# Reordering the opening of a one-core attention and feed-forward kernel: a weight load, two value chunks, two unread products and the banks of the first attention steps

## The chip, the cores and the metric

The kernel runs on one core of one Trainium2 chip. The metric is device time in microseconds from one launch; the time before is the median of three runs. All times inside the kernel are counted from the start of the span of one profiled execution, in which the engines appear as PE (TensorE), DVE (VectorE), ACT (ScalarE), POOL (GpSimd) and SP (the queue that issues stores).

## What is computed

The inputs are q, k and v of 4 batches, 8 heads, 768 positions and 64 channels, an 8 x 8 matrix for each batch and head, and three weights of 512 x 1536, 512 x 1536 and 1536 x 512. Cut to what matters:

```python
for _ in range(5):                      # P: 8 x 8 for each batch and head
    P = exp(P - max); P /= P.sum(-1); P /= P.sum(-2)
k_sorted = einsum('bhij,bhjcd->bhicd', P, k_blocks)   # 8 blocks of 96 rows
v_sorted = einsum('bhij,bhjcd->bhicd', P, v_blocks)
attn = softmax(q_block @ k_sorted_block.T / 8)        # 96 x 96 in each block
x = (attn @ v_sorted_block) as 3072 rows of 512
g = x @ w_gate
out = (g * sigmoid(g)) * (x @ w_val) @ w_out          # 3072 x 512, float32
```

## The kernel before

**The work.** A batch's 768 positions are cut into two halves of 384 rows, so the feed-forward part has eight steps of 384 rows (`ffn(0)` to `ffn(7)`). Each needs an `xt` tile: the attention output of half a batch, transposed, in four slices of 128 (two heads each). The attention of half a batch is four units, numbered 0 to 3 for the first half of batch 0. Unit u consists of

- `qk(0, u)`: eight score products into PSUM (line 332), then the exponentials on ACT (line 345 where one instruction covers both heads, line 343 where there is one for each head);
- `av(0, u)`: eight products of the exponentials with the mixed values (line 359), then on DVE a reciprocal (line 363) and a scaling into the tile `st` (line 365);
- `x_first(u)`: four transposes of `st` on PE (line 376) and a copy into slice u of `xt` (ACT for the first three, DVE for the last).

**Ahead of the units.** The queries, keys and values of batch 0 are transposed and mixed on PE in chunks: `q0_chunk` (line 274), `k0_chunk` (line 284), `v_chunk` (line 300, eight channels at a time for the values). Each chunk's PSUM tile is drained by ACT ("s", line 244) or DVE ("v", line 242). The keys' last chunk (`k0_chunk(32, 16, ...)`) is drained in two parts, the first by ACT for units 0 and 1, the second (`drain_rest`) by DVE for units 2 and 3. The values are first rearranged in SBUF into `vch` by copies on POOL (line 150) and ACT (line 148); POOL's third copy, 64 x 624, fills the channels from 40 up of rows 46 to 71.

**After the units.** `early(n, kcs)` (line 557) computes the first four feed-forward products (two columns of gate, two of value) slice by slice as the slices of `xt` arrive; the rest of `ffn(0)` (lines 410 and 428), the second half of batch 0 and all later batches follow in lists ordered by written-out due times.

**What sets the order.** The order of PE, POOL, DVE and ACT is the order of the calls, written by hand (`manual_schedule`). PE, DVE, ACT and POOL each run their own list in order; semaphores make them wait for each other. POOL issues all loads of this stretch (the DMA queue is fed in the order of its list): values, queries, keys, then the weights (`load_w`, line 136), first 256 columns of `wg` and of `wv`, and so on. A load waits for the landing of the one eight places ahead of it.

**PSUM.** Tags name the places: "a" and "b" are one tile each of two banks, "x" is one bank, and "gen" is three banks in rotation. A new tile of a tag waits until the old one has been read. `qk` with tag "gen" takes two "gen" banks, with "mixed" one "gen" and "x", with "a" or "b" the two-bank tile.

**Unread products.** `fill` (line 477) multiplies 128 x 128 by 128 x 512 zeros into a bank that nobody reads, and `wide_fill` (line 481) does it in float32.

Of the kernel before, what the change touches and what calls it, by code (L numbers as in the profile page):

```python
# [17 lines left out]
def kernel(  # L18
# [24 lines left out]
    TW = 4 * C  # L43
# [6 lines left out]
    wg_dram = moe_w_gate.rearrange("(kc p) f -> p kc f", p=128)  # L50
    wv_dram = moe_w_val.rearrange("(kc p) f -> p kc f", p=128)
# [22 lines left out]
    wg_sb = wpool.tile([128, NKC, DF], BF16)  # L74
    wv_sb = wpool.tile([128, NKC, DF], BF16)
# [59 lines left out]
    def load_w(sb, dram, lo, hi):  # L135
        nc.gpsimd.dma_start(out=sb[:, :, lo:hi], in_=dram[:, :, lo:hi])

    def load_gv(lo, hi):
        load_w(wg_sb, wg_dram, lo, hi)
        load_w(wv_sb, wv_dram, lo, hi)  # L140

    def copy_v(eng, pair, rows, s, n=4, d0=0, d1=D, cs=None):
        cs = cs or slice(s * (C // n), (s + 1) * (C // n))
        dst = vch3[rows, d0:d1, cs]
        src = (dense(v_tiles[0])[rows, cs, d0:d1] if rows == lowr else
               grouped(v_tiles[pair])[rows, s, :, d0:d1])
        if eng is nc.scalar:
            eng.copy(dst, src.transpose([0, 2, 1]))
        else:
            eng.tensor_copy(dst, src.transpose([0, 2, 1]))  # L150
# [16 lines left out]
    def load_q0(t):  # L167
        nc.gpsimd.dma_start(out=q0[t].rearrange("p c d -> p (c d)"), in_=q_runs[0, t])
# [6 lines left out]
        nc.gpsimd.dma_start(out=k0[rows], in_=k_nat[0, :, a * HC:(a + 1) * HC, :])  # L175
    copy_v(nc.gpsimd, 0, lowr, 0)
    copy_v(nc.gpsimd, 0, lowr, 3)
    load_w(wg_sb, wg_dram, 0, 256)
    copy_v(nc.gpsimd, 0, lowr, 0, d0=40, cs=slice(46, 72))
    load_w(wv_sb, wv_dram, 0, 256)  # L180
    load_q0(1)
    load_gv(256, 512)
    load_gv(512, 1024)
# [9 lines left out]
    def vt_tile(pair):  # L193
        if pair not in vts:
            t = vtp.tile([C, 2, H * NB, D + 8], BF16, name=f"vt{pair}", tag="vt")
            nc.vector.memset(t[:, :, :, D:D + 1].rearrange("p u n e -> p (u n) e"), 1.0)
            vts[pair] = t
        return vts[pair]
# [12 lines left out]
    def pair_tile(name, tag):  # L211
        return psum.tile([128, 1024], FP32, name=name, tag=tag)

    def bank_tile(name, tag="gen"):
        return psum.tile([128, 512], FP32, name=name, tag=tag, bufs=3 if tag == "gen" else 1)
# [24 lines left out]
    def drain(eng, dst, src):  # L240
        if eng == "v":
            nc.vector.tensor_copy(dst, src)  # L242
        else:
            nc.scalar.copy(dst, src)  # L244
# [3 lines left out]
    def kqt_tile(b):  # L248
        if b not in kqts:
            kqts[b] = kqp.tile([128, 2 * H2 * NB * C + 32], BF16, name=f"kqt{b}", tag="kqt")  # L250
        return kqts[b]
# [3 lines left out]
    def chunk_tile(name, n, tag):  # L255
        return pair_tile(name, tag) if n == 2 else bank_tile(name, tag)
# [12 lines left out]
    def q0_chunk(t, at, n, eng, tag):  # L269
        dst = kqt_tile(0)[:, GI * C:2 * GI * C].rearrange("p (g t r c) -> p t g r c", g=H2, t=2, c=QC)[:, t]  # L270
        tp = chunk_tile("tq0", n // 8, tag).rearrange("p (l g r) -> p l g r", l=n, g=H2)
        for lc in range(n):
            for two in range(2):
                nc.tensor.matmul(tp[two * D:(two + 1) * D, lc], lhsT=q0[t][:, at + lc, :],  # L274
                                 rhs=sel[:, two], start=True, stop=True)
        drain(eng, dst[:, :, :, at:at + n], tp.rearrange("p l g r -> p g r l"))

    def k0_chunk(at, n, eng, tag, parts=None):
        dst = kqt_tile(0)[:, 0:GI * C].rearrange("p (n a c) -> p a n c", a=2, c=HC)
        rm = rmix[0].rearrange("p a (g two) i -> p two a g i", two=2)  # L280
        tp = chunk_tile("tk0", n // 8, tag).rearrange("p (l a n) -> p l a n", l=n, a=2)
        for lc in range(n):
            for two in range(2):
                nc.tensor.matmul(tp[two * D:(two + 1) * D, lc].rearrange("p a (g i) -> p a g i", g=H2),  # L284
                                 lhsT=k0[:, at + lc, :], rhs=rm[:, two], start=True, stop=True)
        src = tp.rearrange("p l a n -> p a n l")
        if parts is None:
            drain(eng, dst[:, :, :, at:at + n], src)
            return
        drain(eng, dst[:, :, 0:parts, at:at + n], src[:, :, 0:parts])  # L290
        return lambda e: drain(e, dst[:, :, parts:, at:at + n], src[:, :, parts:])

    def v_chunk(b, at, n, eng, tag):
        rows = slice(0, 128) if b % 2 else lowr
        dst = vt_tile(b // 2)[:, b % 2]
        mix = rmix[b][rows, 0].rearrange("p a b -> p (a b)")
        tp = chunk_tile("tv", n // 8, tag).rearrange("p (l n) -> p l n", n=H * NB)
        for ld in range(n):
            col = (at + ld) * C
            nc.tensor.matmul(tp[:, ld, :], lhsT=vch[rows, col:col + 128], rhs=mix,  # L300
                             start=True, stop=True)
        drain(eng, dst[:, :, at:at + n], tp[0:C].transpose([0, 2, 1]))
# [35 lines left out]
    def exps(b, u, wide, pss):  # L338
        n = ecount[0] % 8
        ecount[0] += 2  # L340
        if wide is None:
            for two in range(2):
                nc.scalar.activation(e_all[:, n + two, 0:4 * C], pss[two][0:C, 0:4 * C], AF.Exp, scale=scale)
        else:
            nc.scalar.activation(e_all[:, n:n + 2, 0:4 * C], wide[0:C, :, 0:4 * C], AF.Exp, scale=scale)  # L345
        es[(b, u)] = [e_all[:, n, :], e_all[:, n + 1, :]]

    def qk(b, u, tag="b"):
        exps(b, u, *scores(b, u, tag))

    def av(b, u, tag="a"):
        half, g = divmod(u, H2)
        vt = vts[b // 2][:, b % 2].rearrange("p (h i) e -> p h i e", h=H)
        av_ps = pair_tile("av_ps", tag).rearrange("p (two n) -> p two n", two=2)
        o = av_ps.rearrange("p two (i e) -> p two i e", i=4)
        for two in range(2):
            e = es[(b, u)][two]
            for i4 in range(4):
                nc.tensor.matmul(o[:, two, i4, 0:D + 1], lhsT=e[:, i4 * C:i4 * C + 128],  # L359
                                 rhs=vt[:, 2 * g + two, half * 4 + i4, 0:D + 1],  # L360
                                 start=True, stop=True)
        r_sb = ssp.tile([C, 2, 4, 1], FP32, name="r_sb", tag="r")
        nc.vector.reciprocal(r_sb, o[0:C, :, :, D:D + 1])  # L363
        st = ssp.tile([C, 4, 2, D], BF16, name="st", tag="st")
        nc.vector.tensor_tensor(st.rearrange("p i two d -> p two i d"), o[0:C, :, :, 0:D],  # L365
                                r_sb.to_broadcast([C, 2, 4, D]), op=ALU.mult)
        sts[(b, u)] = st
# [105 lines left out]
    idle_ps = bank_tile("idle_ps", "x")  # L473

    def fill(tile, n):
        for _ in range(n):
            nc.tensor.matmul(tile, lhsT=warm_sb[:, 0:128], rhs=warm_sb, start=True, stop=True)
# [46 lines left out]
    k0_chunk(16, 8, "s", "gen")  # L524
    k0_chunk(24, 8, "v", "gen")
    drain_rest = k0_chunk(32, 16, "s", "a", 2 * NB)
    v_chunk(0, 56, 8, "s", "gen")
    v_chunk(0, 40, 8, "v", "gen")
    qk(0, 0, "b")
    v_chunk(0, 48, 8, "v", "x")  # L530
    drain_rest("v")
    qk(0, 1, "gen")
    av(0, 0, "b")
    qk(0, 2, "a")
    idle_ps = bank_tile("idle_ps", "x")
    fill(idle_ps, 1)
    av(0, 1, "b")
    xts[(0, 0)] = xtp.tile([128, H2, TW], BF16, name="xt0_0", tag="xt")
    qk(0, 3, "gen")

    def x_first(u, eng, tag):
        x_ps = xt_tile(tag, 1)[:, 0]
        x_to(x_ps, 0, u)
        drain(eng, xts[(0, 0)][:, u, :], x_ps.rearrange("p a b -> p (a b)"))

    x_first(0, "s", "gen")
    av(0, 2, "a")
    x_first(1, "s", "gen")
    av(0, 3, "b")
    first = {}  # L550

    def early(n, kcs):
        sb, m, name = ((wg_sb, 0, "g_ps"), (wv_sb, 0, "v_ps"), (wg_sb, 1, "g_ps"), (wv_sb, 1, "v_ps"))[n]
        if n not in first:
            first[n] = (bank_tile(name) if n < 3 else pair_tile(name, "a"))[:, 0:TW]
        for kc in kcs:
            nc.tensor.matmul(first[n], lhsT=sb[:, kc, ts(m, 128)], rhs=xts[(0, 0)][:, kc, :],  # L557
                             start=(kc == 0), stop=(kc == NKC - 1))

    early(0, (0,))  # L560
    early(1, (0,))
    x_first(2, "s", "x")
    early(3, (0,))
    early(2, (0,))
    early(0, (1,))
# [9 lines left out]
    value_out(0, 0, first[1])  # L575
    gate_out(0, 1, first[2])
    value_out(0, 1, first[3])
    q0_chunk(1, 0, 16, "s", "b")
    q0_chunk(1, 16, 8, "v", "x")
    vt_tile(1)  # L580
    nc.vector.tensor_copy(rmix[1][lowr, 1].rearrange("p h i -> p (h i)"), ident[lowr, lowr])
# [114 lines left out]
```

## Time and profile before

| | |
|---|---|
| median of 3 runs | 246.2 us (246.07, 246.2, 247.7) |
| the profiled execution | 245.73 us, of it 244.0 us span |
| mean granted TensorE clock | 0.993 of full |
| PE busy | 233.9 us |
| DVE busy | 155.2 us |
| ACT busy | 112.4 us |
| POOL busy | 54.8 us |

The span runs from the first to the last instruction; 1.73 us of the profiled execution lie outside it. Busy PE time includes the pipeline's own latency and the unread products. In the list of the 40 slices every digit is a tenth, for PEclk a tenth of full clock. The chain is followed back from the last instruction, and the groups give how often an instruction ran, its mean in ns, and what ended the idle time ahead of it.

### The profile page before, as it was taken

To read this page: it belongs to the slowest core of one execution; us is meant where nothing else is said; L and a number is where in the kernel's file an instruction comes from. 1 tells how busy PE (TensorE), PEld (TensorE's weight loads), DVE (VectorE), ACT (ScalarE), POOL (GpSimd) and SP (SyncE) were. 2 spreads that over 40 slices of the span, in tenths; PEclk is the share of its full clock that TensorE was granted. 3 is DMA by queue.
4 is the path that set the end of the run, shared out by engine and by line. 5 is a ranking of instruction groups with operands and counts; after the bars stand their busy time and mean duration, and the time that the engine had idled before them with its cause. 6 is when DMAs were issued, how large, how long until landed. Compare 5 with 4: busy or idle time off the path is not lost.

```text
span 244.0 us, 5910 instructions
## 1 busy us (share of the span) xinstructions
PE 233.9 (96%) x2468; PEld 137.6 (56%) x2490; DVE 155.2 (64%) x326; ACT 112.4 (46%) x190; POOL 54.8 (22%) x66
## 2 busy tenths in 40 slices
PE   7779999999999999999999999999999999999994
PEld 3376566676555565555555565565556555555543
DVE  6786699876664585867755845574675576445700
ACT  3985654476635444455543452254325334332312
POOL 5998228970006089000000000000000000000000
PEclk9997999999999999999999999999999999999999
DMA  5999999999926998644121212012111211110122
GB/s 97 211 133 188 207 210 211 206 204 196 171 79 98 219 172 101 130 80 95 46 75 35 60 58 77 2 59 63 32 43 46 75 36 43 43 43 3 43 86 86
DMA packets 40698, 24.76 MB, mean 102 GB/s; under 512 B 29408, under 2 KB 35424, under 8 KB 40672
## 3 DMA queue, kind: packets, MB, share of 16 engines
q0 software_dynamic: 20688, 14.16, 40.3%
q1 hardware_dynamic: 19840, 10.17, 15.9%
q8 instruction: 19, 0.31, 0.5%
q10 hardware_dynamic: 144, 0.07, 0.1%
q14 instruction: 7, 0.06, 0.1%
HBM read 28.32 MB, written 7.86 MB: 148 GB/s over the span
## 4 chain that ended last, share of the span: by engine, by line
PE 89%; DMA 4%; DVE 3%; issue 1%; POOL 1%; ACT 0%; DVEq 0%; POOLq 0%
PE v_ps L428 25%; PE g_ps L410 25%; PE o_ps L445 24%; DMA qk<-in_k_dram 4%; PE av_ps L359 3%; PE tkq L264 3%; PE qk L332 3%; PE tv L310 1%; PE o_ps L461 1%; PE tv L300 1%; PE tk L284 1%; PE x_ps L376 1%; DVE h L433 1%; PE g_ps L557 1%; PE v_ps L557 1%
## 5 line engine op out<-in xcount | busy, mean ns | idle before, releaser
L420 DVE SCALAR_TENSOR_TENSOR gs_sb<-th_sb,g_ps 128x384 bf16<-128x384 bf16 x96 | 53.1, 553 | 50.4 <-ACT th_sb L418 47.3
L428 PE MATMUL v_ps<-xt,wv_sb 128*128 128x384 bf16 x376 | 76.5, 326 | 0.5 <-DVE gs_sb L420 0.5
L410 PE MATMUL g_ps<-xt,wg_sb 128*128 128x384 bf16 x376 | 76.6, 325 | 0.1
L418 ACT ACTIVATE th_sb<-g_ps 128x384 bf16<-128x384 f32 x96 | 47.1, 491 | 57.5 <-PE g_ps L410 54.7
L445 PE MATMUL o_ps<-wo,h 128*128 128x512 bf16 x254 | 61.4, 379 | 1.5 <-issue 0.5
L433 DVE SCALAR_TENSOR_TENSOR h<-v_ps,gs_sb 128x384 bf16<-128x384 f32 x96 | 53.4, 556 | 8.2 <-PE tq L274 0.5
L428 PEld LDWEIGHTS <-wv_sb 128*128 128x128 bf16 x376 | 35.1, 97 | 23.5 <-issue 0.7
L410 PEld LDWEIGHTS <-wg_sb 128*128 128x128 bf16 x376 | 34.8, 97 | 23.4
L445 PEld LDWEIGHTS <-h 128*128 128x128 bf16 x276 | 26.0, 98 | 28.5
L450 ACT COPY o_sb<-o_ps 128x512 f32<-128x512 f32 x23 | 13.5, 586 | 49.3 <-PE o_ps L445 49.3
L150 POOL COPY vch<-v 64x1536 bf16<-64x1536 bf16 (+2 forms) x11 | 29.5, 2720 | 9.9 <-PE g_ps L410 8.1
L345 ACT ACTIVATE e_all<-qk 96x768 bf16<-96x768 f32 x30 | 23.3, 801 | 4.1 <-PE qk L332 4.1
L365 DVE TENSOR_TENSOR st<-av_ps,r_sb 96x512 bf16<-96x512 f32 x32 | 21.8, 681 | 0.3
L359 PEld LDWEIGHTS <-e_all 96*128 96x128 bf16 x256 | 12.4, 100 | 5.3 <-ACT e_all L345 0.6
L359 PE MATMUL av_ps<-vt,e_all 96*128 96x65 bf16 x256 | 13.5, 196 | 0.8 <-DVE vt L242 0.5
L244 ACT CAST vt<-tv 96x1024 bf16<-96x1024 f32 (+1 forms) x10 | 9.7, 966 | 4.2 <-PE tv L310 3.5
L363 DVE RECIPROCAL r_sb<-av_ps 96x8 f32<-96x8 f32 x32 | 6.4, 199 | 8.2 <-PE av_ps L359 8.2
L242 DVE CAST vt<-tv 96x512 bf16<-96x512 f32 (+1 forms) x9 | 8.1, 920 | 2.6 <-PE tv L310 1.8
L481 PE MATMUL idle_ps<-wide_sb 128*128 128x512 f32 x10 | 7.2, 866 | 1.5 <-DVE wide_sb L70 1.5
L242 DVE COPY oq_v<-o_ps 128x128 f32<-128x128 f32 x1 | 0.3, 292 | 9.3 <-PE o_ps L461 9.3
L395 POOL DMA_DIRECT2D q_scr<-in_q_dram x2 | 5.6, 2810 | 0.3 <-issue 0.3
L332 PE MATMUL qk<-kqt 64*128 64x96 bf16 x128 | 4.7, 208 | 0.4 <-DVE kqt L242 0.2
(87 smaller groups left out, 131.7 us busy)
## 6 DMA issues: line engine op xcount, KB each, us to landing
out_dram<-o_sb SPq DMA_DIRECT2D x23, 256.0 KB, 2.0
v<-in_v_dram POOLq DMA_DIRECT2D x4, 384.0 KB, 11.9
wo<-in_moe_w_out_dram POOLq DMA_DIRECT2D x3, 512.0 KB, 16.0
kqp<-in_k_dram POOLq DMA_DIRECT2D x2, 768.0 KB, 9.6
q_scr<-in_q_dram POOLq DMA_DIRECT2D x2, 768.0 KB, 17.4
v<-in_v_dram POOLq DMA_DIRECT2D x2, 768.0 KB, 9.8
wg_sb<-in_moe_w_gate_dram POOLq DMA_DIRECT2D x2, 512.0 KB, 11.8
wv_sb<-in_moe_w_val_dram POOLq DMA_DIRECT2D x2, 512.0 KB, 14.5
```

Of the source, the lines that this page charges most:

```text
L150: eng.tensor_copy(dst, src.transpose([0, 2, 1]))
L332: nc.tensor.matmul(pss[two][:, i4 * C:(i4 + 1) * C], lhsT=k_sb[lo:lo + D, k_at + at:k_at + at + 128], rhs=q_sb[lo:lo + D, q_at + at:q_at + ...
L345: nc.scalar.activation(e_all[:, n:n + 2, 0:4 * C], wide[0:C, :, 0:4 * C], AF.Exp, scale=scale)
L359: nc.tensor.matmul(o[:, two, i4, 0:D + 1], lhsT=e[:, i4 * C:i4 * C + 128], rhs=vt[:, 2 * g + two, half * 4 + i4, 0:D + 1], start=True, sto ...
L365: nc.vector.tensor_tensor(st.rearrange("p i two d -> p two i d"), o[0:C, :, :, 0:D], r_sb.to_broadcast([C, 2, 4, D]), op=ALU.mult)
L410: nc.tensor.matmul(g_ps, lhsT=wg_sb[:, kc, ts(m, 128)], rhs=xt[:, kc, :], start=(kc == 0), stop=(kc == NKC - 1))
L418: nc.scalar.activation(th_sb, g_ps, AF.Tanh, scale=0.5)
L420: nc.vector.scalar_tensor_tensor(gs_sb, th_sb, 1.0, g_ps, op0=ALU.add, op1=ALU.mult)
L428: nc.tensor.matmul(v_ps, lhsT=wv_sb[:, kc, ts(m, 128)], rhs=xt[:, kc, :], start=(kc == 0), stop=(kc == NKC - 1))
L433: nc.vector.scalar_tensor_tensor(h_tiles[n][:, m, :], v_ps, 0.5, gs_tiles.pop(m), op0=ALU.mult, op1=ALU.mult)
L445: nc.tensor.matmul(o_ps, lhsT=h_w[:, m, ts(t3, 128)], rhs=wo_sb[part][:, m % 4, :], start=(m == 0), stop=(m == NFC - 1))
L450: nc.scalar.copy(o_sb, o_ps)
```

## The change

Five edits, all in the first 30 us of the program:

1. The load of the first 256 columns of `wv` is issued ahead of POOL's third value copy (it was issued behind it).
2. `v_chunk(0, 40, ...)`, drained by DVE, comes ahead of `v_chunk(0, 56, ...)`, drained by ACT.
3. Two more unread products, 128 x 512 bf16, stand between `qk(0, 1)` and `av(0, 0)`, in a "gen" bank.
4. `qk(0, 2)` goes from "a" to two "gen" banks, `qk(0, 3)` from "gen" to "mixed".
5. `av(0, 1)` goes from "b" to "a", `av(0, 2)` from "a" to "b", `av(0, 3)` from "b" to "a"; the fourth early product goes from "a" to "b", and the next query chunk from "b" to "a".

```diff
     copy_v(nc.gpsimd, 0, lowr, 0)
     copy_v(nc.gpsimd, 0, lowr, 3)
-    load_w(wg_sb, wg_dram, 0, 256)
+    load_gv(0, 256)
     copy_v(nc.gpsimd, 0, lowr, 0, d0=40, cs=slice(46, 72))
-    load_w(wv_sb, wv_dram, 0, 256)
     load_q0(1)
...
     drain_rest = k0_chunk(32, 16, "s", "a", 2 * NB)
+    v_chunk(0, 40, 8, "v", "gen")
     v_chunk(0, 56, 8, "s", "gen")
-    v_chunk(0, 40, 8, "v", "gen")
     qk(0, 0, "b")
     v_chunk(0, 48, 8, "v", "x")
     drain_rest("v")
     qk(0, 1, "gen")
+    fill(bank_tile("idle_ps"), 2)
     av(0, 0, "b")
-    qk(0, 2, "a")
+    qk(0, 2, "gen")
     idle_ps = bank_tile("idle_ps", "x")
     fill(idle_ps, 1)
-    av(0, 1, "b")
+    av(0, 1, "a")
     xts[(0, 0)] = xtp.tile([128, H2, TW], BF16, name="xt0_0", tag="xt")
-    qk(0, 3, "gen")
+    qk(0, 3, "mixed")
...
     x_first(0, "s", "gen")
-    av(0, 2, "a")
+    av(0, 2, "b")
     x_first(1, "s", "gen")
-    av(0, 3, "b")
+    av(0, 3, "a")
...
-            first[n] = (bank_tile(name) if n < 3 else pair_tile(name, "a"))[:, 0:TW]
+            first[n] = (bank_tile(name) if n < 3 else pair_tile(name, "b"))[:, 0:TW]
...
-    q0_chunk(1, 0, 16, "s", "b")
+    q0_chunk(1, 0, 16, "s", "a")
     q0_chunk(1, 16, 8, "v", "x")
```

`load_gv(lo, hi)` calls `load_w` for `wg` and then for `wv`.

## The prediction

> **What bounds the kernel now.** I read the page first: PE has hardly a gap, and the chain that ended last is PE almost throughout. The one flaw is in the fourth slice of the granted clock.
>
> ```profile
> PE 233.9 (96%) x2468; PEld 137.6 (56%) x2490; DVE 155.2 (64%) x326; ACT 112.4 (46%) x190; POOL 54.8 (22%) x66
> ...
> PEclk9997999999999999999999999999999999999999
> ...
> PE 89%; DMA 4%; DVE 3%; issue 1%; POOL 1%; ACT 0%; DVEq 0%; POOLq 0%
> ```
>
> So from some 24 us on PE sets the end, and a step that comes there earlier moves the whole rest earlier by as much, as long as loads and copies keep up. The change lies ahead of that. Second view, stretches of 3.41 us (columns: stretch, length, busy us and count of PE, PEld, DVE, ACT, POOL, then clock, DMA share, GB/s):
>
> ```profile
> 6.23:9.64 3.41, 2.43 (x6) 0.76 (x5) 2.56 (x13) 3.35 (x5) 3.33 (x2) 1.00 1.07 214
> 9.64:13.05 3.41, 3.01 (x117) 2.30 (x117) 2.58 (x9) 3.07 (x3) 3.41 (x3) 1.00 0.92 187
> 13.03:16.44 3.41, 2.75 (x125) 2.46 (x120) 2.63 (x5) 2.69 (x5) 3.41 (x5) 1.00 0.88 103
> 16.44:19.85 3.41, 2.29 (x53) 1.68 (x53) 2.77 (x5) 2.91 (x6) 3.41 (x6) 1.00 1.21 194
> 19.85:23.26 3.41, 3.41 (x41) 2.63 (x41) 2.58 (x6) 2.00 (x5) 3.01 (x22) 0.50 1.32 179
> ```
>
> The clock is halved for exactly one such stretch, right after the one in which PE was least busy (2.29 us; with 2.43 or more in a stretch the next one kept full clock). Third view, PE in order of time, which shows where those gaps are (start, duration, idle before and its releaser):
>
> ```profile
> 17.01 0.39 PE L332 MATMUL qk<-kqt 64*128 64x96 bf16 x8
> 17.95 0.40 PE L359 MATMUL av_ps<-vt,e_all 96*128 96x65 bf16 x8 [0.55 <-DVE vt L242]
> 18.55 0.34 PE L332 MATMUL qk<-kqt 64*128 64x96 bf16 x8 [0.20 <-DVE kqt L242]
> 18.83 0.39 PE L477 MATMUL idle_ps<-warm_sb 128*128 128x512 bf16 x1
> 19.48 0.40 PE L359 MATMUL av_ps<-vt,e_all 96*128 96x65 bf16 x8 [0.26 <-DVE st L365]
> ```
>
> The chain of waits says the same: ACT and DVE stand behind PE's gaps here, and from 19.48 to 25.71 the chain is PE without a break, most of it at half clock.
>
> ```profile
> 17.21 0.69 DVE vt L242
> 17.90 0.60 DVE kqt L242
> ...
> 18.64 0.70 DVE st L365
> ...
> 19.48 0.40 PE av_ps L359 x8
> ```
>
> **The change, part by part.**
>
> *Load of `wv` ahead of the third copy.* POOL's rows: issue of `wg` 11.87 to 12.65, copy 12.65 to 13.92, issue of `wv` 13.84 to 14.60. Now the issue comes at 12.65 and the copy at 13.42 to 14.69. The copy's first reader, the value chunk at 15.85, has 1.1 us to spare; `q0` and the later issues keep their times (the same two pieces of work stand ahead of them). Landing of `wv` (4.4 us after issue, at 18.2) moves to about 17.1; its reader stands at 22.06 before and, below, at 21.1, so it is hidden either way. The keys land at 13.7, and `wv`'s issue ends at 13.4; the `wg` load issued 0.8 us ahead of it already stood behind the keys without a visible cost. Worth 0.
>
> *Value chunk order.* DVE's two value drains start at 16.52 and 17.21. The first can now start at 16.29 (its products are done 0.24 earlier). The second needs the products of 16.78 to 17.17, which stand behind `qk(0, 0)` at 16.60, which waits for ACT's key drain (15.96 to 16.55). So it starts at 17.21 as before: 0. ACT's own value drain comes 0.08 later, the exponentials of unit 0 end at 17.88 instead of 17.80, still ahead of DVE's drain at 17.90.
>
> *Two products.* They start at 17.2 (their bank is free at 17.11) and take 0.60 (row L477 at 10.31: two in 0.60), to 17.8, inside the gap that ends at 17.95. Cover left: 0.1. At half clock two would take some 1.0 and push `av(0, 0)` by 0.3; the row at full clock is nearest, so 0. What they buy is the clock: below.
>
> *Banks.* `av(0, 1)` waited for the scaling of unit 0 (ends 19.34) because both used "b". In "a" it needs DVE's second key drain (18.50) and the exponentials of unit 1 (18.26 and 18.64), so it follows the unread product directly: 18.83 + 0.22 = 19.05, 0.43 earlier. `qk(0, 2)` waits for DVE's key drain (18.50) in any banks: 18.55 as before; its exponentials become two of 0.48 (0.86 for the pair, row L343) instead of one of 0.81: +0.04. `qk(0, 3)` finds "mixed" free and follows at 19.29 (19.81).
>
> *The steps after that, clock at full.* I carry the rows forward, with PE to ACT or DVE 0.04, back to PE 0.06 (0.1 where the scaling releases the transposes), and each engine in its order:
>
> | | before | after | what it then waits for |
> |---|---|---|---|
> | unit 1 scaled (DVE) | 20.85 | 20.42 | `av(0, 1)` |
> | unit 3 exponentials end | 21.21 | 20.53 | ACT in order |
> | first transposes | 20.24 | 19.47 | exponentials of unit 2, first half |
> | unit 2 scaled | 22.16 | 21.31 | DVE in order |
> | second `xt` copy ends | 22.03 | 21.35 | ACT in order |
> | unit 3 scaled | 22.99 | 22.19 | DVE in order |
> | third transposes | 22.38 | 21.41 | unit 2 scaled |
> | fourth transposes | 23.63 | 22.32 | unit 3 scaled, third copy |
> | fourth `xt` copy ends | 24.36 | 23.05 | DVE |
> | last early product starts | 25.39 | 24.08 | seven products at 0.16 |
>
> Sum: **-1.3 us**. Of it about 0.5 comes from the banks alone (`qk(0, 3)` 0.52 earlier, after which PE is the chain in both), 0.8 from the clock. The ends: -0.5 if the clock falls as before, and for the clock alone at most half of 3.41, 1.7, which DVE and ACT in the table cut to 0.8.
>
> *Does the clock stay?* In the stretch 16.44 to 19.85 the gaps close: 0.55 to 0.1 by the products, 0.26 to 0 by the bank. Busy goes from 2.29 to about 3.0, above the 2.43 and 2.75 that kept it. In the next stretch the table leaves PE one gap, 20.13 to 20.50, so 3.0 again. Shifted edges make it worse: 17.4 to 20.8 holds 0.1, 0.2 and 0.4 of gaps, 2.75, still a value that kept the clock. In another execution the edges can lie elsewhere, so this is likely, not sure.
>
> The Trainium skill, page "TensorE: Matmul & The Clock Gate", section "Why this matters for your kernels", says that only PE gaps over about 3 us bring the half clock back. By that, gaps of 0.55 us would not be the cause, the products would cure nothing, and the sum would be -0.5 (rival 1). The trace disagrees: the clock fell with no gap over 0.55 us ahead of it.
>
> *Does the gain arrive?* Weights: the second half-load of `wv` (columns 512 on) is issued at 17.34 and lands 12.2 later, 29.5; its reader moves from 31.27 to 30.0. The next pair lands at 35.7 for a reader at 37.9, then 36.6. The narrowest is POOL's rearrangement of batch 1's values:
>
> ```profile
> 38.33 11.29 POOL L150 COPY vch<-v 64x1536 bf16<-64x1536 bf16 x4
> ...
> 51.09 0.63 PE L300 MATMUL tv<-rmix,vch 128*128 128x64 bf16 x16
> ```
>
> It ends at 49.62 and starts after a load lands, not after PE; the reader moves from 51.09 to 49.8. The gain just passes, and about 1.4 us is the cap there (1.7 if the earlier `wv` brings the later loads forward by 0.3).
>
> **Rivals.**
>
> 1. *The clock falls in the same place.* For it: one execution shows one fall, and 2.43 against 2.29 is a narrow mark. Against: busy 3.0. Then only the banks count: -0.5, 245.7.
> 2. *The clock falls one stretch later* (slower). If the gap at 20.13 to 20.50 and the short transposes leave too little work, the half clock lies on 23.3 to 26.7, where PE is busy without a pause (3.41 of 3.41 in that stretch): +1.7 against -1.3, +0.4, 246.6. It decides when busy in 19.85 to 23.26 drops under 2.43; I have 3.0. The same page, section "Part 1: The HAM clock gate", says that the window runs free of the kernel's start; no single execution can show that.
> 3. *The moved steps find another wait*, and the change does not do what it says: ACT, in order, has 0.86 of exponentials for each of three units in a row, and DVE 0.9 for each `av`; if these are already the bound, nothing moves: 246.2. Against it: ACT idles 0.39, 0.60 and 0.92 between 18.5 and 23, and DVE 0.59 and 0.38.
>
> **How the numbers follow.** The profiled execution took 245.73 (244.0 of span), 0.5 under the median 246.2. The sum gives 244.4 on its own time and 244.9 on the median, and I give 244.9. Chances: forecast 0.66, rival 1 0.19, rival 2 0.10, rival 3 0.05. The forecast's own range is 244.1 (1.6 off the profiled time) to 245.4 (gain 0.8). The range to hold 8 in 10 takes in rivals 1 and 3: 244.1 to 246.3. All cases lie within 1% (243.7 to 248.7, about what a measurement of this kernel can tell from no change): 0.91. Faster needs 2.5 us, more than the cap of 1.7: 0.05. Slower by 2.5 us needs the clock to fall twice or a load to come late: 0.04.
>
> **What would show it.** Right: granted clock 1.00 from 6.2 us to the end; `av(0, 1)` at about 19.05, right behind the unread product; the fourth `xt` copy ending near 23.05; the query chunk (L273) near 24.3; PE's later order the same, 1.3 us earlier; span near 242.7. Wrong: a 0.50 stretch anywhere (rivals 1, 2); `av(0, 0)` later than 18.1 (products too long); PE idle ahead of batch 1's first value chunk, released by POOL; the first value chunk later than 15.9, released by POOL's third copy.

## The result, and the profile after

The changed kernel takes **245.47 us** in the median (22 runs, 244.16 to 249.71), the kernel before on the same chip 246.6 us (22 runs, 245.32 to 248.55). The ratio is 0.9945 [0.9919, 0.997]; it leaves out the changed kernel's three longest runs (248.45 us and more), which count as disturbed, and with them the two medians give 0.9954. The forecast was 244.9 us, 1.3 us under the kernel before; 1.1 us were measured. The profiled execution took 244.4 us with a span of 242.6 (the prediction had 244.4 on its own time and 242.7).

The page of the changed kernel, the granted clock in 40 slices:

```profile
PEclk9999999999999999999999999999999999999999
```

The 7 in the fourth slice is gone. The stretches of the changed kernel, first two counted from this execution's own rise to full clock (at 7.6 us; more on that rise below), then one with the edges of the weak stretch before (columns: stretch, length, busy us and count of PE, PEld, DVE, ACT, POOL, then clock, DMA share, GB/s):

```profile
14.42:17.84 3.42, 2.97 (x106) 2.22 (x99) 2.59 (x5) 2.74 (x6) 3.42 (x6) 1.00 1.32 188
17.84:21.25 3.41, 2.93 (x60) 2.22 (x59) 3.14 (x9) 3.05 (x8) 3.21 (x7) 1.00 1.28 182
...
16.44:19.85 3.41, 3.04 (x65) 2.05 (x64) 2.94 (x7) 3.05 (x8) 3.41 (x6) 1.00 1.19 189
```

PE is busy 2.9 to 3.0 us in each, where 3.0 was forecast, and the clock stays at 1.00. (Busy figures of PE can be a little low: in the other traces the pages count some 2470 products for some 2490 weight loads, so a few products have no record. In this trace both counts are 2492.) PE in order of time, changed kernel (line numbers are one lower than before):

```profile
17.30 0.61 PE L476 MATMUL idle_ps<-warm_sb 128*128 128x512 bf16 x2
17.96 0.40 PE L358 MATMUL av_ps<-vt,e_all 96*128 96x65 bf16 x8
18.57 0.34 PE L331 MATMUL qk<-kqt 64*128 64x96 bf16 x8 [0.20 <-DVE kqt L241]
18.84 0.39 PE L476 MATMUL idle_ps<-warm_sb 128*128 128x512 bf16 x1
19.07 0.41 PE L358 MATMUL av_ps<-vt,e_all 96*128 96x65 bf16 x8
...
24.30 0.95 PE L273 MATMUL tq<-sel,qk 128*64 128x64 bf16 x48
```

The two unread products fill 17.30 to 17.91, and `av(0, 0)` starts at 17.96 (17.95 before): hidden. `av(0, 1)` starts at 19.07 instead of 19.48, with no wait on `st`. The query chunk starts at 24.30; before, it was 25.64, so this execution is 1.34 us ahead there, and its span is 1.4 us shorter.

One trace is one execution. The mean granted clock of each run tells more: 1.00 means that the clock never fell ("held"), about 0.99 that it lay at half for some 3.4 us, 0.986 or less for longer. Runs in each class, with the median us (the chips are called A, B and C; that of the 22 runs is not on record):

| kernel | runs | held | one fall | more |
|---|---|---|---|---|
| before, chip A | 35 | 2 (245.53) | 14 (246.03) | 19 (247.37) |
| before, chip B | 31 | 3 (244.92) | 14 (245.93) | 14 (247.13) |
| before, chip C | 11 | 0 | 3 (246.42) | 8 (247.30) |
| changed | 22 | 12 (244.53) | 6 (246.61) | 4 (248.47) |
| changed, chip C | 6 | 4 (245.04) | 0 | 2 (247.5) |

So the change moves the share of runs that hold from 5 of 77 to 16 of 28. It doesn't make every run hold. Held times are compared on one chip only, since the same kernel can hold at 244.30 us on one and at 244.84 on another (the kernel with four wide products, below). The question for the experiments is which edit does which, and what the remaining falls are.

### The profile page after: what moved, and what is told of

It is laid out like the page before. It is cut to its first block, busy times and chain, and to the rows that moved or that the text cites. A ratio compares the mean times of both kernels' runs of the same rounds, so it can differ in the third digit from the quotient of the medians.

```text
span 242.6 us, 5936 instructions
## 1 busy us (share of the span) xinstructions
PE 234.8 (97%) x2492; PEld 136.7 (56%) x2492; DVE 155.1 (64%) x326; ACT 112.3 (46%) x191; POOL 54.8 (23%) x66
## 4 chain that ended last, share of the span: by engine, by line
PE 90%; DMA 4%; DVE 3%; POOL 1%; issue 1%; ACT 0%; DVEq 0%; POOLq 0%
PE v_ps L427 25%; PE o_ps L444 25%; PE g_ps L409 25%; DMA qk<-in_k_dram 4%; PE av_ps L358 3%; PE tkq L263 3%; PE qk L331 3%; PE tv L309 1%; PE o_ps L460 1%; PE tv L299 1%; PE tk L283 1%; DVE h L432 1%; PE g_ps L557 1%; DVE gs_sb L419 1%; PE x_ps L375 1%
## 5 line engine op out<-in xcount | busy, mean ns | idle before, releaser
L444 PE MATMUL o_ps<-wo,h 128*128 128x512 bf16 x276 | 64.4, 379 | 0.0
L344 ACT ACTIVATE e_all<-qk 96x768 bf16<-96x768 f32 x29 | 22.5, 801 | 3.7 <-PE qk L331 3.7
L358 PE MATMUL av_ps<-vt,e_all 96*128 96x65 bf16 x256 | 13.0, 193 | 0.1
L148 ACT COPY vch<-v 64x640 bf16<-64x640 bf16 (+2 forms) x3 | 4.8, 1602 | 0.2 <-DMA v<-in_v_dram 0.2
```

The lines of the kernel that those rows point to most:

```text
L444: nc.tensor.matmul(o_ps, lhsT=h_w[:, m, ts(t3, 128)], rhs=wo_sb[part][:, m % 4, :], start=(m == 0), stop=(m == NFC - 1))
```

## The experiments

**Theory.** The clock falls after a stretch with too little PE work; the two products put the work there, the new banks shorten the path by 0.5 us, and the other edits do nothing. **Rivals:** the banks close enough of the gap by themselves, and the products are idle work; or the earlier load of `wv` gives the gain; or the falls come from somewhere else altogether.

### One part taken away or done alone

Changed kernel without the two products:

```diff
-    fill(bank_tile("idle_ps"), 2)
     av(0, 0, "b")
```

> The changed kernel without the two unread products; the load order, the value chunk order and the new banks stay. Theory 1 (the clock falls after a stretch of 3.41 us in which PE had too little to do): the 0.5 us gap ahead of av(0, 0) is open again, busy time in the sparsest stretch drops back to about 2.6 us, the clock falls in nearly every run, and only the 0.5 us of the banks is left: 0.998 of the kernel before. Theory 2 (gaps this short do not touch the clock, the products are idle work): as fast as the changed kernel, 0.9945 of the kernel before, with the clock falling as often as there.

Measured: 244.77 us, ratio 0.995 [0.9918, 0.9983]; of 12 runs 7 held (244.51), 3 had one fall (246.6), 2 more. The theory, which had the clock fall in nearly every run, fails here: without the products the kernel holds about as often as with them (16 of 28, on other chips). A stretch of this trace:

```profile
15.85:19.26 3.41, 2.35 (x64) 1.99 (x64) 2.77 (x5) 3.04 (x7) 3.41 (x6) 1.00 1.19 190
```

PE busy is 2.35, hardly more than the 2.29 after which the clock fell before, and the clock held. On the same chip, A, 2 of 35 runs of the kernel before held, so the edits that are left (banks, load order, chunk order) do something for the clock.

Kernel before, with the two products alone:

```diff
+    fill(bank_tile("idle_ps"), 2)
     av(0, 0, "b")
```

> The kernel before with nothing but the two unread products ahead of av(0, 0). Theory 1: the 0.55 us gap closes, the 0.26 us gap ahead of av(0, 1) stays, busy in the sparsest stretch is about 2.7 us, and the clock holds in part of the runs; in those the span is about 0.8 us shorter than before (243.2), av(0, 1) still at 19.48. Mean about 0.998 of the kernel before. Theory 2: nothing moves, 1.000, clock 0.993 as before.

Measured: 245.25 us, ratio 0.9972 [0.9946, 0.9998]; 8 of 12 held (245.02), 4 had one fall (246.72). So the products alone raise the held share too, from 2 of 35. Held runs are 0.4 to 0.55 us longer than those of the three kernels with new banks on this chip (244.47 to 244.61): the banks' share of the sum.

Changed kernel with the load of `wv` back behind the third copy:

```diff
-    load_gv(0, 256)
+    load_w(wg_sb, wg_dram, 0, 256)
     copy_v(nc.gpsimd, 0, lowr, 0, d0=40, cs=slice(46, 72))
+    load_w(wv_sb, wv_dram, 0, 256)
```

> The changed kernel with the wv load issued behind the third value copy again. If the load order is worth nothing, as I costed it: as fast as the changed kernel (0.9945 of the kernel before); the first wv load lands at 18.2 instead of 18.1 and the later loads 0.5 to 1.9 us later (the changed kernel had them that much earlier than before), POOL's copies of batch 1 end near 49.6 instead of 48.0, and their reader at about 49.8 waits at most 0.1. If the earlier loads carry part of the gain: 0.2 to 0.5 us slower than the changed kernel, with PE idle ahead of batch 1's first value chunk or ahead of a weight.

Measured: 244.99 us, ratio 0.9948 [0.9916, 0.9981]; 7 of 12 held (244.47), 4 one fall (246.62), 1 more. The held time is that of the kernel without the products on the same chip (244.51, with the load moved), so the load order is worth nothing that these runs could show. This trace caught one of the falls. PE in order of time at its start, then its stretches:

```profile
1.47 4.45 PE L481 MATMUL idle_ps<-wide_sb 128*128 128x512 f32 x6 [1.47 <-DVE wide_sb L70]
7.79 0.17 PE L484 MATMUL idle_ps<-vch 64*8 64x8 bf16 x1 [1.87 <-ACT vch L148]
7.88 3.55 PE L481 MATMUL idle_ps<-wide_sb 128*128 128x512 f32 x4
```

```profile
4.75:8.16 3.41, 1.54 (x5) 0.55 (x4) 2.29 (x12) 1.90 (x4) 1.68 (x1) 1.00 1.01 199
8.16:11.57 3.41, 3.35 (x9) 0.90 (x10) 2.43 (x11) 3.23 (x3) 3.41 (x2) 0.50 1.06 214
...
14.98:18.39 3.41, 1.97 (x98) 1.75 (x91) 1.92 (x4) 1.72 (x4) 3.41 (x6) 1.00 1.18 146
```

The fall is not where the prediction looked. The chip starts the program at a low clock and rises at a time that varies. The clock column does not show this start (it reads 1.00 from 0 us); the products' durations do: in the trace of the changed kernel one float32 instruction takes 1.06 us ahead of the rise and 0.59 us behind it. The three wide products are six such instructions. Here they took 4.45 us, in the traces of before and after 5.17 and 5.49 (the earlier the rise, the shorter). After an early rise the three wide products end at 5.92, PE idles 1.87 us until the values' first copy, the stretch holds 1.54 us of work, and the next 3.41 us run at half clock (the four instructions at 7.88 take 3.55 us; 1.98 in the trace of before). The last row is a stretch with 1.97 us of work after which the clock stayed.

Changed kernel with four more unread products:

```diff
+    fill(bank_tile("idle_ps", "x"), 2)
     k0_chunk(0, 8, "s", "x")
...
-    fill(bank_tile("idle_ps"), 2)
+    idle_gen = bank_tile("idle_ps")
+    fill(idle_gen, 2)
     av(0, 0, "b")
+    fill(idle_gen, 1)
     qk(0, 2, "gen")
...
     av(0, 2, "b")
+    fill(bank_tile("idle_ps"), 1)
     x_first(1, "s", "gen")
```

> The changed kernel with four more unread products in gaps that its trace still shows: two ahead of the first key chunk (gap 0.44), one ahead of qk(0, 2) (0.20), one ahead of x_first(1) (0.22). Theory 1: the changed kernel's single runs show a mean clock of 1.00 in some and 0.99 in others, since the edges of the stretches differ; with the gaps closed nearly all runs have 1.00, the best times stay near 244.2, and the median falls by 0.5 to 1 us, to 0.991 of the kernel before. Theory 2: the share of runs with a fallen clock stays about a half, and the time is that of the changed kernel or up to 0.3 longer where a product delays what stands behind it.

Measured: 244.73 us, ratio 0.9945 [0.9918, 0.9972]; 10 of 12 held (244.61), 2 had one fall. More than 16 of 28, but a share of 12 runs can't be read closely, and two falls remain.

### The early gap made smaller too

One more wide product ahead of the values' copy (`wide_fill(3)` to `wide_fill(4)`) takes from the early gap. With it, the two products can be judged with fewer early falls. First the changed kernel with four:

```diff
-    wide_fill(3)
+    wide_fill(4)
```

> The changed kernel with four instead of three wide float32 products at the start. In the trace of e3 the clock rose at 4.8 us, the three products ended at 5.7, PE then had nothing until 7.6, and the clock fell from 8.2 to 11.6. Theory 1 (the falls that the changed kernel still has in 10 of 22 runs are of that kind: an early rise ends the wide products early): the fourth product fills that gap, at least 10 of 12 runs hold a mean clock of 0.997 or more, median 244.5, 0.991 of the kernel before. Rival (they come from the sparse stretch between 13 and 20 us): the share stays near one half, 0.994.

Measured: 244.29 us, ratio 0.9906 [0.9873, 0.9938]; **8 of 8 held**. Its PE at the start and two of its stretches:

```profile
1.47 5.97 PE L480 MATMUL idle_ps<-wide_sb 128*128 128x512 f32 x8 [1.47 <-DVE wide_sb L70]
7.58 0.17 PE L483 MATMUL idle_ps<-vch 64*8 64x8 bf16 x1
```

```profile
6.08:9.49 3.41, 3.27 (x9) 1.05 (x7) 2.53 (x13) 3.25 (x5) 3.24 (x2) 1.00 1.06 213
16.32:19.73 3.41, 2.94 (x70) 2.22 (x71) 2.94 (x7) 3.06 (x7) 3.41 (x6) 1.00 1.12 174
```

In this trace no wait stands ahead of the small product at 7.58 any more: the fourth wide product ends just there. That depends on the rise. In four of the seven traces with four wide products a wait of 0.36 to 1.06 us is left there, and in one with a late rise (at 7.65 us; the kernel with the old chunk order, below) the fourth product ends late and the small one starts at 8.15.

The same without the two products (the removal of the first experiment and this line together):

> As e5, without the two unread products of the change. With the early falls out of the way this tells what the two products do. If they hold the clock in the stretch from 16.4 us, as I forecast: clear falls near 19 us come back in a third of the runs or more, and the median is 0.5 to 1 us above that of e5. If the new banks alone close enough of the gaps: the same share and the same time as e5, within 0.2 us.

Measured: 245.3 us, ratio 0.9958 [0.9927, 0.999]; 4 of 12 held (244.62), 6 one fall (245.71), 2 more. With 8 of 8 against 4 of 12 on one chip, the products do hold the clock once the fourth wide product is there.

The kernel before with four wide products:

> The kernel before with four instead of three wide products. Its own runs have two falls of the clock (mean clock 0.985, 247.4 us) in about half the cases, one (0.993, 246.05) in 14 of 35. Theory 1: the early fall goes, the one at 19.9 us stays; nearly all runs have one fall, median 246.1, 0.997 of the kernel before. Rival: no effect, half of the runs with two falls.

Measured: 246.42 us, ratio 0.9986 [0.9953, 1.0018]; 3 of 12 held (244.78), 3 one fall (246.15), 6 more. I had put the longer falls of the kernel before down to the early gap beside the later one. That idea falls: they go on with the fourth wide product, and this trace, of 246.68 us, shows one:

```profile
15.61:19.02 3.41, 2.44 (x58) 1.78 (x57) 2.78 (x6) 2.98 (x6) 3.41 (x6) 1.00 1.14 172
19.02:22.43 3.41, 3.25 (x44) 2.66 (x45) 2.14 (x7) 2.10 (x5) 3.17 (x22) 0.50 1.33 185
22.43:25.84 3.41, 3.41 (x19) 1.85 (x17) 0.80 (x2) 0.60 (x2) 1.20 (x3) 0.50 1.25 207
```

One fall can last two stretches: after 3.25 us of work in a half-clock stretch the clock did not come back, after 3.41 it did.

All extra products and four wide:

> e4 (four more unread products in the gaps at 13.2, 18.4 and 20.3 us) with the fourth wide product as well. Theory 1: all runs hold the clock, median 244.6; the products of e4 cost 0.1 in runs that hold it, so it is level with e5 or 0.1 slower where e5 holds everywhere, and faster in the mean where e5 still has falls.

Measured: 244.97 us, ratio 0.9938 [0.9912, 0.9964]; 12 of 12 held, at 244.97, where the kernel with two products and four wide holds at 244.30 on the same chip. The four more products keep nothing that the two don't. The held run is 0.67 us longer, though 0.1 was expected; with three wide products, on chip A, the same four cost 0.1 (244.61 against 244.47 and 244.51).

### Repeats, and the last two edits

The changed kernel once more, on chip C:

> The changed kernel as it is, beside the three others on one chip. Expected as in its own 22 runs: about half of the runs with a mean clock of 0.997 or more near 244.5, the others 2 us longer or more; 0.9945 of the kernel before in the median.

Measured: 245.25 us, ratio 0.9947 [0.9901, 0.9993]; 4 of 6 held (245.04), 2 had more than one fall. Its trace caught one of these. PE at the key chunk, then the stretches:

```profile
13.66 1.59 PE L283 MATMUL tk<-rmix,qk 128*64 128x64 bf16 x89 [0.34 <-DMA qk<-in_k_dram]
16.63 0.29 PE L283 MATMUL tk<-rmix,qk 128*64 128x64 bf16 x7 [1.39 <-issue]
```

```profile
15.51:18.92 3.41, 1.94 (x48) 1.47 (x49) 1.56 (x4) 1.96 (x4) 3.41 (x6) 1.00 1.22 193
18.92:22.33 3.41, 3.38 (x48) 2.59 (x49) 2.35 (x5) 2.34 (x7) 3.17 (x22) 0.50 1.33 180
```

PE stalled 1.39 us after 89 of 96 key products, waiting for nothing that the profile shows. That left 1.94 us of work in the stretch, in spite of the two products, and half clock followed for two stretches (to 25.74). One of the two products has no record in this trace, so the true figure may be some 0.2 us higher.

The kernel with four wide products once more:

> The changed kernel with four wide products at the start, once more, beside the changed kernel itself. If the fourth product takes the early fall away: no run under 0.997, 0.991 of the kernel before, below the changed kernel by the share of its runs with a fall times 2 us, that is 0.8 to 1 us in the mean. If e5's 8 runs were chance: falls in some of the runs.

Measured: 244.84 us, ratio 0.9905 [0.9874, 0.9935]; 6 of 6 held. Its median is under that of the changed kernel on this chip (245.25), and all 14 of its runs on two chips held, so it is the version to keep; the intervals of the two ratios overlap.

The same with the value chunks in their old order:

```diff
+    v_chunk(0, 56, 8, "s", "gen")
     v_chunk(0, 40, 8, "v", "gen")
-    v_chunk(0, 56, 8, "s", "gen")
```

> e5 with the two value chunks in the old order. As I costed it the order is worth nothing, since DVE's second drain starts at 17.21 either way: level with e5 within 0.2 us, DVE's two drains back to back, av(0, 0) at the same distance from the first key chunk. If the earlier first drain counts: 0.2 to 0.7 us slower.

Measured: 244.87 us, ratio 0.9908 [0.9877, 0.9939]; 6 of 6 held. The held time is level with 244.84: the chunk order is worth nothing that these runs could show. DVE of this kernel, then of the changed kernel:

```profile
16.91 1.38 DVE L241 CAST vt<-tv 96x512 bf16<-96x512 f32 x2 [0.86 <-PE tv L299]
```

```profile
16.30 0.69 DVE L241 CAST vt<-tv 96x512 bf16<-96x512 f32 x1 [0.56 <-PE tv L299]
17.22 0.69 DVE L241 CAST vt<-tv 96x512 bf16<-96x512 f32 x1 [0.23 <-PE tv L299]
```

The trace of the old order runs some 0.4 us later from the key chunk on (14.02 instead of 13.72). In it the two drains stand back to back; in the new one the first is earlier and DVE idles 0.23 us before the second, which still starts at 17.22 (17.21 before).

Last, the kernel with four wide products and the old banks:

```diff
-    qk(0, 2, "gen")
+    qk(0, 2, "a")
...
-    av(0, 1, "a")
+    av(0, 1, "b")
...
-    qk(0, 3, "mixed")
+    qk(0, 3, "gen")
```

(and `av(0, 2)`, `av(0, 3)`, the fourth early product and the next query chunk back likewise).

> e5 with the old tags of qk(0, 2), qk(0, 3), av(0, 1) to av(0, 3), the fourth early product and the query chunk; load order, chunk order, two products and four wide products stay. With the clock held the banks are worth 0.5 us by my sum (av(0, 1) waits for the scaling of unit 0 again, 0.4 later): held runs 0.5 us above e5. By the stretch rule the 0.26 gap comes back and some runs may fall. If the banks' worth was only in the clock: held runs level with e5.

Measured: 245.41 us, ratio 0.9933 [0.9902, 0.9964]; 6 of 6 held. Against 244.84 on the same chip, in held runs alone, the banks are worth 0.57 us (the lowest of the six, 245.16, is above the highest of the other six, 245.02). PE in order of time, old banks first, then the new ones:

```profile
19.00 0.34 PE L331 MATMUL qk<-kqt 64*128 64x96 bf16 x8 [0.20 <-DVE kqt L241]
19.27 0.39 PE L476 MATMUL idle_ps<-warm_sb 128*128 128x512 bf16 x1
19.92 0.40 PE L358 MATMUL av_ps<-vt,e_all 96*128 96x65 bf16 x8 [0.26 <-DVE st L364]
```

```profile
18.40 0.34 PE L331 MATMUL qk<-kqt 64*128 64x96 bf16 x8 [0.20 <-DVE kqt L241]
18.68 0.39 PE L476 MATMUL idle_ps<-warm_sb 128*128 128x512 bf16 x1
18.90 0.41 PE L358 MATMUL av_ps<-vt,e_all 96*128 96x65 bf16 x8
```

From `qk(0, 2)` to `av(0, 1)` it is 0.92 us in the old banks and 0.50 in the new: with the wait on `st` gone, `av(0, 1)` comes 0.42 sooner, against the 0.43 of the prediction.

With four wide products, the two edits in question make a table of two by two (runs that held of all runs; the upper row is from chip B, the lower left from C, the lower right from both):

| | old banks | new banks |
|---|---|---|
| without the two products | 3 of 12 | 4 of 12 |
| with them | 6 of 6 | 14 of 14 |

Here the products hold the clock and the banks don't. With three wide products the picture is another one: products alone 8 of 12, banks with the load and chunk order 7 of 12, all of them 16 of 28, none 5 of 77. Why the banks help there (7 of 12 against 2 of 35 on chip A) and not with four wide products (4 of 12 against 3 of 12 on B) stays open.

## Why the prediction was right, and where it was not

**Load order, 0:** right (held runs on chip A 244.47 with it back, 244.51 with it moved). A step on the way was wrong: the first load of `wv` landed at 18.06, not 17.1 (18.21 before), so the earlier issue gained 0.15 us and not 1.1.

**Chunk order, 0:** right, for the reason given. The second drain starts at 17.22, the first 0.22 earlier.

**Two products hidden:** right, 0.05 us of cover left instead of 0.1.

**Banks, 0.5:** right, 0.57 measured. Seven of the ten rows in the table of later steps came within 0.05 us, among them third transposes 21.39 (21.41 forecast), unit 2 scaled 21.28 (21.31), fourth transposes 22.29 (22.32) and the end of the fourth `xt` copy 23.02 (23.05). Three were further off: first transposes 19.68 instead of 19.47, unit 3's exponentials end at 20.65 instead of 20.53, and unit 3 scaled 22.12 instead of 22.19. Nothing later was moved by them.

**Clock, 0.8:** right as the price of the fall that the traced execution of before had: runs of the kernel before with one fall are 0.50 and 1.01 us above its held ones (few of these: 2 and 3). Wrong as a picture of the kernel before, where the usual case is a longer fall (41 of 77 runs), and of the changed kernel, where a run with one fall costs 2.1 us over a held one (246.61 against 244.53). That is more than the 1.7 that the prediction had as the most. The trace with the load back, also of 246.61 us, shows where it comes from, at the stall in the key chunk (changed kernel, then load back):

```profile
15.64 0.29 PE L283 MATMUL tk<-rmix,qk 128*64 128x64 bf16 x7 [0.33 <-issue]
```

```profile
17.83 0.29 PE L284 MATMUL tk<-rmix,qk 128*64 128x64 bf16 x7 [1.28 <-issue]
```

This place is 2.19 us later, and so is the query chunk (26.49 against 24.30). The key chunk started 0.90 us later behind the half clock, lost 0.35 in a wait on its way, and 0.95 by the longer stall. So a good part of that price is the stall and not the half clock itself, as far as one trace shows.

From trace to trace, with one fall before and none after, the sum is right (span 1.4 us shorter). That it also fits the medians is in part luck, since two errors offset each other: the gain against the commoner longer falls is larger, and the changed kernel holds less often than forecast.

**Does the clock stay, chance 0.66:** 16 of 28 runs, 0.57. The step that was off is the claim that the stretch around 17 to 20 us is the only weak one. Two others were not seen: the gap ahead of the values' first copy, which counts when the clock rises early, and the stall in the key chunk. The mark of 2.43 does not hold either. Over all 14 traces, in stretches of 3.41 us from the first rise on, the clock fell after busy 1.55, 1.94, 2.29 and 2.45 us, and was kept after 1.97, 2.09, 2.18, 2.22, 2.35 (twice), 2.41, 2.42, 2.43 and 2.49; with more than that it was always kept (the program's last stretch left out). So under 2.5 it fell four times and stayed ten times: little busy time is a sign of a weak stretch, and what decides there stays open. The longest gap doesn't decide it either: the clock fell behind gaps of 0.55 us and stayed behind gaps of 1.28 and 1.33. That the two products do raise the held share is shown by runs (4 of 12 against 8 of 8 on one chip), and not by this mark.

**The Trainium skill's rule** (page "TensorE: Matmul & The Clock Gate", section "Why this matters for your kernels") is that only gaps over about 3 us lose the clock. Measured against it are falls whose longest gap ahead was 0.55 us (before), 1.39 (the changed kernel's second trace) and 1.87 (load back). By that rule the two products would be idle work; 4 of 12 against 8 of 8 held shows that they are not. The same page of the Trainium skill, section "Part 1: The HAM clock gate", says that the window runs free of the kernel. The traces agree: the first rise, worked out from the float32 instructions, lies between 4.65 and 7.65 us, each of the four falls starts one or four times 3.41 us behind it, and falls last one or two times 3.41 us.

**Rivals.** The first (fall in the same place, 245.7) fits the kernel with new banks, four wide products and no two: 245.71 in its runs with one fall. With three wide products such runs took 246.6. The second (a fall in another place, 246.6) was given 0.10; 6 of 28 runs of the changed kernel had one fall and took 246.61 in the median, the forecast's price; that is luck, since the places that the traces show, and the terms of the price, are other ones than I had named. The third (nothing moves) is refuted by the rows of the changed kernel: `av(0, 1)` 0.41 us and the query chunk 1.34 us earlier.

**The cap of 1.4 us:** mis-sized. POOL's copies of batch 1's values and their reader, changed kernel:

```profile
36.78 11.23 POOL L150 COPY vch<-v 64x1536 bf16<-64x1536 bf16 x4
```

```profile
49.76 0.63 PE L299 MATMUL tv<-rmix,vch 128*128 128x64 bf16 x16
```

They end at 48.01, 1.75 us ahead of the reader, where 49.62 had been carried over. The loads came earlier by up to 2 us (a `wv` load at 33.8 instead of 35.7). Over all traces the copies start at 36.72 to 38.33 with the old load order (four traces) and at 36.04 to 38.12 with the new one (ten): the start moves by itself, and the load order is not shown to have brought it.

## What to carry to other kernels

Ask for the granted clock of every run before trusting one trace: one execution showed one weak stretch, and the others showed two more. Here neither the two products nor the fourth wide one held the clock in every run by itself. All kernels with the two products and four wide ones held in 38 of 38 runs; with the two products and three wide it was 41 of 64, with four wide and without the two products 7 of 24. For the changed kernel the fourth wide product took the held share from 16 of 28 to 14 of 14, and the ratio from 0.9945 [0.9919, 0.997] to 0.9906 [0.9873, 0.9938]. A tile given a free bank was worth the wait that it drops (0.42 us at the place, 0.57 at the end), since PE, which waited, is the bound from there on.

## What the chip showed that I had not expected

**A fall can last two stretches.** Four traces show a fall. Two of them lasted one stretch (before, load back) and two lasted two (before with four wide products, the changed kernel's second trace). In the first half-clock stretch PE was busy 3.41 and 3.35 us where the clock came back, and 3.25 and 3.38 where it did not. 3.35 and 3.38 stand in the wrong order for a mark, so what ends a fall stays open.

**PE can stall inside a row of small products, and always at the same place in its list.** In 8 of 14 traces PE stood still 0.21 to 1.39 us in the key chunk, put down to "issue" (0.22 before, 0.33 in the changed kernel); in two more it is 0.13. The place is 89 products into the chunk with three wide products. Where two more instructions stand ahead of it (a fourth wide product, or the two more `fill` products), it is 87. So in each of these ten traces it lies behind the 223rd weight load of PE's list. The end of the stall follows the landing of a 16 KB transfer of the instruction queue, by 1.20 to 1.48 us in all ten (landed at 14.15 and ended at 15.63 before; 15.24 and 16.63 in the changed kernel's second trace). That looks like PE waiting for its next instructions; no experiment moved the transfer or the loads beside it on purpose, so it stays a likely cause and not a shown one. With four wide products the longest stall of seven traces is 0.80 us, with three it is 1.39, so the held share that the fourth brings need not come from the early gap alone.

**Unread products may not be free just because they fit.** Four more of them lengthened held runs by 0.67 us on chip B (244.97 against 244.30) and by 0.1 on chip A, where the gaps seemed to have room for all but 0.1 us. Why the two differ stays open.
